# A kernel that plans its own instruction order: casting-queue loads planned to land later, and a longer hold ahead of the next score tile

## The chip, the cores and the metric

One core of one Trainium2 chip. The metric is the device time of one execution in microseconds (us), given as a median over several executions. Engines: PE is TensorE, ACT is ScalarE, DVE is VectorE, POOL is GpSimd, SP is SyncE. A number after an L is a line of the kernel; the change adds one line near the top, so L630 of the kernel before is L631 of the changed one.

## The reference

```python
# q, k, v: (8 batches, 12 heads, 448, 64); x: (3584, 768); w_in: (768, 2048); w_out: (2048, 768); float32
scores = matmul(q, k.T) / 8 - log(448)
attn   = 1 / (1 + exp(-scores))
x      = matmul(attn, v)  # heads put side by side: 3584 x 768
h      = x @ w_in
g      = 0.5 * h * (1 + tanh(sqrt(2/pi) * (h + 0.044715 * h**3)))
out    = g @ w_out
```

## The kernel before

The kernel holds a small scheduler. While it is built, it simulates the engines and the DMA queues with durations of its own, picks at each moment which operation an engine begins next, and then emits one fixed instruction stream for each engine, with semaphores. What the model believes about a load therefore decides the order on the engines, but never when the load really lands. The parts that matter:

```python
DMA_TAIL = 1200.0                      # ns, in the model
...
def drain(self, t):                    # the model's DMA: when a load has landed
    ...
    op.end = self.moved + self.DMA_TAIL + op.late
...
HOLD = 200.0
...
def pe_next(self, t):                  # what PE begins next (first stretch, cut)
    if can and left <= 1 and ...:      # 1. a score tile, if a pair of PSUM banks is free
        return make_qk(n, t)
    soon = trans_ready(t) and ...
    if m and not soon and ...:         # 2. a tile of attention times v
        return av_take(1, t)[0]
    ends = [...]                       #    ends of the ACT tiles under way
    if 0 < n < UB and can and ends and min(ends) < t + HOLD:
        return None                    #    batch 0 only: wait, a bank comes free soon
    if trans_ready(t):                 # 3. the transposes of a q or k
        return make_trans(t)
    return make_part(...) if ...       # 4. a pair of early MLP matmuls
```

Work comes in groups of four heads; three groups are a batch. Groups 0 and 1 load q and k as float32 through the queues of SP and ACT, and DVE or ACT casts them to bf16. From group 2 to group 5 they come through the casting queue of POOL (all loads of v, w_in and w_out too), which converts while it moves. For group 1:

```python
ld[g] = plan.add(Op("ld%s%d" % (nm, g), "AQ" if (nm, g) == ("q", 1) else "SP",
                    lambda e, ap=ap, d=dst[s]: e.dma_start(d[:], ap), ...,
                    pkt=(16, 89.0), late=LATE if g >= PE_TR * NG + NG else 0.0))   # group 1: late = 0
...
cast: deps [ld[g]] + ...               # kb <- kf, qb <- qf
freed[key] = Op("trp%s%s" % (nm, key), "PE", fn, [eye, cast[key], bank_free[bank]], ...)   # transposes
```

The transposes of group 1 stand at a fixed place in PE's stream, between score tiles of group 0. If the load of k for group 1 ("k1" below) is late, PE stops there, and ACT soon has no score tile left.

## Time and profile before

| | before |
|---|---|
| first three runs | median 388.91 us (388.79 to 390.27) |
| the profiled run | 388.43 us, span 386.6 us |
| ACT's 21 sigmoid tiles of batch 0 | 7.06 to 24.65 us |
| run of 24 MLP matmuls in batch 1, start | 55.47 (chain), 55.31 (timeline) |

The chain and the timeline date the same instruction some 0.15 us apart; below, a difference is always taken within one view. The profile itself is read in the prediction.

### The profile page before, as it was taken

What the parts mean: (1) busy time and instruction counts of PE and PEld (TensorE: products, weight loads), DVE (VectorE), ACT (ScalarE), POOL (GpSimd) and SP (SyncE); (2) the same over time, 40 slices, a digit from 0 to 9 for tenths busy, and PEclk for the clock granted to TensorE, in tenths of its full rate; (3) what the DMA queues carried; (4) which work ended last, traced back from release to release, by engine and by line L of the source; (5) the groups of instructions that cost most, each with busy time, mean ns of one, the idle gap of its engine ahead of it and who ended that gap; (6) DMA issues with size and microseconds to landing.
All of it is one profiled execution on the core that took longest, in us unless ns stands there. A gap on an engine that the chain in (4) does not pass through costs nothing.

```text
span 386.6 us, 7500 instructions
## 1 busy us (share of the span) xinstructions
PE 381.8 (99%) x3210; PEld 202.5 (52%) x3210; DVE 155.9 (40%) x273; ACT 227.6 (59%) x337; POOL 53.6 (14%) x84
## 2 busy tenths in 40 slices
PE   8999999999999999999999999999999999999996
PEld 6434445545555555555555555554555545555565
DVE  3446623147680085602864057710767016400000
ACT  5999962268564576546755476645856467543221
POOL 6994110001010111001110011100201000000000
PEclk9999999999999999999999999999999999999999
DMA  8999999747784068903779049940779501110133
GB/s 232 189 203 203 210 207 319 115 88 185 185 209 88 26 164 219 219 0 109 157 203 199 1 120 205 230 72 0 185 184 216 81 0 42 43 41 2 41 83 81
DMA packets 64225, 51.74 MB, mean 134 GB/s; under 512 B 36288, under 2 KB 60736, under 8 KB 64192
## 3 DMA queue, kind: packets, MB, share of 16 engines
q1 hardware_dynamic: 48928, 36.81, 38.9%
q0 software_dynamic: 14560, 13.64, 22.2%
q10 hardware_dynamic: 704, 0.82, 0.7%
q8 instruction: 25, 0.41, 0.4%
q14 instruction: 8, 0.07, 0.1%
HBM read 45.61 MB, written 11.01 MB: 146 GB/s over the span
## 4 chain that ended last, share of the span: by engine, by line
PE 95%; ACT 3%; DVE 0%; issue 0%
PE ps L822 39%; PE ps L777 36%; PE ps L630 9%; PE ps L678 7%; ACT at L641 3%; PE ps L753 2%; PE ps L434 1%; PE ps L587 1%; ACT th L650 0%; PE ps L584 0%; DVE at L654 0%; ACT xT L360 0%; DVE qT L361 0%; ACT ob L360 0%; DVE gT L426 0%
## 5 line engine op out<-in xcount | busy, mean ns | idle before, releaser
L650 ACT ACTIVATE th<-ps 128x896 f32<-128x896 f32 x147 | 126.8, 929 | 44.9 <-PE ps L630 44.8
L822 PE MATMUL ps<-w_out,gT 128*128 128x384 bf16 (+2 forms) x912 | 152.9, 324 | 0.1
L654 DVE TENSOR_SCALAR at<-th 128x896 bf16<-128x896 f32 x147 | 92.2, 628 | 126.3 <-ACT th L650 125.5
L777 PE MATMUL ps<-xT,w_in 128*128 128x448 bf16 x738 | 143.2, 353 | 0.0
L822 PEld LDWEIGHTS ps<-w_out,gT 128*128 128x128 bf16 x912 | 85.9, 98 | 65.5 <-ACT th L650 5.9
L791 ACT ACTIVATE gT<-ps 128x448 bf16<-128x448 f32 x128 | 69.6, 549 | 79.5 <-PE ps L777 78.6
L777 PEld LDWEIGHTS ps<-xT,w_in 128*128 128x128 bf16 x738 | 71.3, 98 | 68.6 <-issue 3.4
L630 PE MATMUL ps<-qT,kT 64*64 64x448 bf16 x672 | 48.3, 359 | 0.5 <-ACT at L641 0.4
L510 POOL DMA_DIRECT2D vb<-in_v_dram x24 | 14.8, 616 | 236.7 <-PE ps L630 233.7
L678 PE MATMUL ps<-at,vb 64*64 64x448 bf16 x672 | 38.2, 350 | 0.2 <-DVE xT L361 0.2
L361 DVE COPY ob<-ps 128x384 f32<-128x384 f32 x43 | 23.8, 554 | 25.1 <-PE ps L822 24.2
L630 PEld LDWEIGHTS ps<-qT,kT 64*64 64x64 bf16 x672 | 15.6, 105 | 25.1 <-issue 11.9
L678 PEld LDWEIGHTS ps<-at,vb 64*64 64x64 bf16 x672 | 19.4, 107 | 12.1 <-issue 1.1
L360 ACT ACTIVATE ob<-ps 128x384 f32<-128x384 f32 (+2 forms) x14 | 6.6, 468 | 25.4 <-PE ps L822 25.4
L361 DVE CAST xT<-ps 128x448 bf16<-128x448 f32 x27 | 16.6, 623 | 10.9 <-PE ps L678 10.9
L512 POOL DMA_DIRECT2D vb<-in_v_dram x24 | 18.8, 785 | 0.2 <-issue 0.2
L641 ACT ACTIVATE at<-ps 128x896 bf16<-128x896 f32 x21 | 17.5, 926 | 0.6 <-PE ps L630 0.5
L361 DVE CAST kb<-kf 128x896 bf16<-128x896 f32 (+2 forms) x21 | 12.6, 599 | 11.4 <-DMA kf<-in_k_dram 10.9
L360 ACT ACTIVATE xT<-ps 128x448 bf16<-128x448 f32 x21 | 11.6, 551 | 1.9 <-PE ps L678 1.9
L361 DVE CAST qb<-qf 128x896 bf16<-128x896 f32 (+1 forms) x20 | 12.2, 608 | 0.7 <-DMA qf<-in_q_dram 0.6
L886 POOL DMA_DIRECT2D w_in<-in_moe_w_in_dram x16 | 10.2, 719 | 0.0
L753 PE MATMUL ps<-xT,w_in 128*128 128x448 bf16 x30 | 7.4, 355 | 0.0
(31 smaller groups left out, 48.2 us busy)
## 6 DMA issues: line engine op xcount, KB each, us to landing
out_dram<-ob SPq DMA_DIRECT2D x54, 192.0 KB, 2.9
kf<-in_k_dram SPq DMA_DIRECT2D x19, 448.0 KB, 4.4
qf<-in_q_dram SPq DMA_DIRECT2D x18, 448.0 KB, 5.6
vb<-in_v_dram POOLq DMA_DIRECT2D x48, 112.0 KB, 5.1
w_out<-in_moe_w_out_dram POOLq DMA_DIRECT2D x4, 768.0 KB, 21.3
w_in<-in_moe_w_in_dram POOLq DMA_DIRECT2D x12, 192.0 KB, 11.3
kb<-in_k_dram POOLq DMA_DIRECT2D x4, 224.0 KB, 8.5
qb<-in_q_dram POOLq DMA_DIRECT2D x4, 224.0 KB, 8.9
```

What stands on the lines that cost most here:

```text
L360: return e.activation(o, i, AF.Copy)
L361: return e.tensor_copy(o, i)
L512: c = plan.add(Op("ldv%db" % g, "SWQ", lambda e, d=dst[64:128], ap=hi: e.dma_start(d, ap), deps, 610.0, 0.0, prio=order_v(g), sem="ldv%db" ...
L630: r = mm(ps[64 * half:64 * half + 64, (x, y)[a], 0:S], kv[d, a, j, :], qv[d, a, :, :], start=True, stop=True)
L641: lambda e: e.activation(at[as_][:], both, AF.Sigmoid, bias=bias, scale=scale),
L650: lambda e: e.activation(th[ts][:], both, AF.Tanh, bias=0.5 * bias, scale=0.5 * scale),
L654: lambda e: e.tensor_scalar(at[as_][:], th[ts][:], 0.5, 0.5, op0=ALU.mult, op1=ALU.add),
L678: r = mm(ps[64 * c:64 * c + 64, banks[a], 0:S], vb[s][d, slot, j, :], at[as_][d, a, :], start=(j == 0), stop=(j == NJ - 1))
L753: r = mm(ps[:, bank, 0:S], w_in[:, kt, fc * 128:(fc + 1) * 128], xT[b][:, kt, :], start=(kt == 0), stop=(kt == KT - 1))
L777: r = mm(ps[:, bank, 0:S], w_in[:, kt, fc * 128:(fc + 1) * 128], xT[xb][:, kt, :], start=(kt == 0), stop=(kt == KT - 1))
L791: lambda e: e.activation(gT[:, fc, col:col + S], ps[:, bank, 0:S], AF.Gelu_apprx_tanh),
L822: r = mm(ps[:, bank, 0:hi - lo], gT[:, fc, col:col + 128], w_out[:, fc, lo:hi], start=(fc == 0), stop=(fc == FC - 1))
```

## The change

It tunes two of the planner's beliefs: loads on the casting queue are taken to land 0.9 us later (so that PE is not planned onto data that is only just there), and in batch 0 PE begins nothing long within 0.3 us of the next free score bank.

```diff
     LATE2 = 500.0
+    LATE3 = 900.0
...
-    HOLD = 200.0
+    HOLD = 300.0
...
-   prio=order_q(g), sem="ldb%s%d" % (nm, s), pkt=(16, 72.0)))
+   prio=order_q(g), sem="ldb%s%d" % (nm, s), pkt=(16, 72.0), late=LATE3))
...     # the same "late=LATE3" on both halves of each v load, and on the w_in and w_out loads
```

More of the change, by code (lines that the diff above doesn't have):

```diff
@@ L510, in load_v @@
             a = plan.add(Op("ldv%da" % g, "SWQ", lambda e, d=dst[0:64], ap=lo: e.dma_start(d, ap),
-                            deps, 610.0, 0.0, prio=order_v(g), sem="ldv%da" % s, pkt=(8, 72.0)))
+                            deps, 610.0, 0.0, prio=order_v(g), sem="ldv%da" % s, pkt=(8, 72.0), late=LATE3))
             c = plan.add(Op("ldv%db" % g, "SWQ", lambda e, d=dst[64:128], ap=hi: e.dma_start(d, ap),
-                            deps, 610.0, 0.0, prio=order_v(g), sem="ldv%db" % s, pkt=(8, 72.0)))
+                            deps, 610.0, 0.0, prio=order_v(g), sem="ldv%db" % s, pkt=(8, 72.0), late=LATE3))
             ld_v[g] = (a, c)
@@ L878, in load_w_in @@
                     w_in_x.append(plan.add(Op("wx%d" % c, "SWQ", lambda e, d=dst, s_=src: e.dma_start(d, s_),
-                                              [], 620.0, 0.0, prio=(1, EARLY.index("x0")), sem="wx%d" % c, pkt=(8, 95.0))))
+                                              [], 620.0, 0.0, prio=(1, EARLY.index("x0")), sem="wx%d" % c, pkt=(8, 95.0), late=LATE3)))
             for c in range(2):
@@ L887, in load_w_in @@
                                            after, 620.0, 0.0, prio=prio,
-                                           sem="wi%d.%d.%d" % (n, c, a), pkt=(12, 80.0) if n else (8, 95.0))))
+                                           sem="wi%d.%d.%d" % (n, c, a), pkt=(12, 80.0) if n else (8, 95.0), late=LATE3)))
             w_in_ld[n] = ops
@@ L894, in load_w_out @@
                                        lambda e: e.dma_start(w_out[:, n * FC // 4:(n + 1) * FC // 4, :], src),
-                                       after, 760.0, 0.0, prio=prio, sem="wo%d" % n, pkt=(32, 117.0)))]
+                                       after, 760.0, 0.0, prio=prio, sem="wo%d" % n, pkt=(32, 117.0), late=LATE3))]
         state = {"n": 0, "av": 0, "queue": [], "a": (0, 0), "b": 0, "h": 0, "avj": 0, "burst": False, "run": 0, "last": ""}
```

## The prediction

> **What bounds the kernel now.** I read the page first, then the chain that ended last in order of time, then each engine's share by stage, then the timelines of ScalarE (ACT) and TensorE (PE) in the first 60 us. The page puts almost the whole span on PE. The windows show that this is not so in the first 20 us.
>
> ```profile
> PE 95%; ACT 3%; DVE 0%; issue 0%
> ...
> 7.00:20.40 13.40, 12.87 (x215) 6.30 (x209) 6.70 (x13) 13.25 (x17) 13.40 (x23) 1.00 1.22 199
> 20.40:55.10 34.70, 34.59 (x367) 15.01 (x368) 19.20 (x32) 31.64 (x48) 15.44 (x23) 1.00 1.21 206
> 55.10:386.60 331.50, 328.55 (x2588) 177.08 (x2586) 127.86 (x223) 180.24 (x270) 21.52 (x30) 1.00 0.54 122
> ```
>
> The columns of the last three lines are stretch, length, then the busy time of PE, weight loads, DVE, ACT and POOL. From 7.0 to 20.4 us ACT is busy 13.25 of 13.40: it makes the sigmoid tiles of batch 0 (line 641, 21 tiles of 128x896), and each needs a score tile (line 630, four matmuls) that PE must have made. From 20.4 us to the end PE is the limit. The chain in order of time (start, us, what) says where it changes hands:
>
> ```profile
> 7.06 5.01 ACT at L641 x6
> 12.06 0.14 issue
> 12.20 0.38 PE ps L630 x4
> 12.58 0.19 PE ps L678 x4
> 12.77 0.51 PE ps L587 x14
> 13.29 0.31 PE ps L630 x4
> 13.60 0.19 PE ps L678 x4
> 13.79 0.51 PE ps L587 x14
> 14.30 0.34 PE ps L630 x4
> 14.64 0.02 issue
> 14.66 5.80 ACT at L641 x7
> 20.46 0.04 issue
> 20.51 0.38 PE ps L630 x4
> ```
>
> Twice in it a score tile (L630) stands behind 14 transposes (L587) of q or k, and ACT then waits for that tile. How much in all:
>
> ```profile
> 7.06 17.59 ACT L641 ACTIVATE at<-ps 128x896 bf16<-128x896 f32 x21 [0.49 <-PE ps L630]
> ```
>
> Narrow windows on this row give the single starts. Undisturbed sigmoids start 0.80 apart. Numbered s0 to s20, s0 starts at 7.06 and s20 at 23.73, so 20 steps took 16.67; at 0.80 they would take 15.96. ACT therefore loses about 0.7 us to late score tiles. The losses sit at s5 (start 11.14, 0.08 late), s8 (13.65, 0.10), s9 (14.66, 0.21), s14 (18.73, 0.06) and s20 (23.73, 0.19). The last one is not a transpose but a pair of early MLP matmuls (L753, 0.48 with the switch) ahead of the tile:
>
> ```profile
> 22.52 0.36 PE L678 MATMUL ps<-at,vb 64*64 64x448 bf16 x4
> 22.81 0.55 PE L753 MATMUL ps<-xT,w_in 128*128 128x448 bf16 x2
> 23.29 0.38 PE L630 MATMUL ps<-qT,kT 64*64 64x448 bf16 x4
> ```
>
> **What the Trainium skill says.** "Perfetto Trace Analysis", Optimization Strategy, says that the contended engine can change between regimes and that one looks for the gaps of that engine inside its regime; the same page, Identifying the Most-Contended Engine, says that matmul busy time is no good measure. The trace agrees: PE shows 12.87 of 13.40 busy in a stretch where it waits for ACT. "TensorEngine Tiling (Array Packing)", Key Properties, says that a change of tiling mode drains TensorE. Here six MLP matmuls before a score tile take 1.24 us in the chain and twelve take 2.38, so six cost 1.14 (0.19 each) and the change of mode costs the 0.10 left over; starts of single matmuls put it at 0.094. "DMA: Bandwidth & Descriptors", Anatomy of one DMA, gives about 2 us fixed per load and says most of it is completion; here the page has 5.1 us (median) from issue to landing for the v loads, as up to four dozen loads queue. No run yet shows whether a later assumed landing is nearer the truth.
>
> **The change, part by part.** Nothing that runs is added or removed on purpose: the kernel plans its own order at build time, and the change moves two numbers of that plan. LATE3 lets the plan believe that each load on the casting queue lands 0.9 us later, and HOLD (200 to 300 ns) forbids PE to begin a transpose or an early MLP pair in batch 0 when an ACT tile will end, and so free a score bank, within 0.3 us. I compared the instruction order of the two programs. DMA queues: identical. DVE and ACT: one tanh tile moves past gelus early in batch 1, and likewise at its end; one affine step moves across an eviction. PE: the rows differ from the 16th to the 88th; after that the order is the same to the last instruction, that is from 55.12 us on. So LATE3 does nothing to loads after that point, and only the first 55 us can change. There the new order (a) puts one more warm-up matmul (+0.05) where the first attention-times-v tile stood; (b) makes the score tiles of s9, s10 (one before the q transposes instead of both after), s14 and s16 go ahead of the transposes; (c) takes the MLP pair out from ahead of the tile of s20; (d) merges runs of MLP matmuls, with 50 instead of 52 changes of mode by the 55 us point (counted row by row).
>
> Working through it with durations from the trace (score or attention tile 0.19, change of mode 0.094, 14 transposes with change 0.51, sigmoid 0.80 apart and 0.92 long, a score tile 0.43 to 0.44 before its sigmoid):
> - s5: its tile follows the warm-up directly, at 10.57; s5 at 11.06 instead of 11.14.
> - s8: the k transposes still stand ahead of its tile; it stays 0.10 late, at 13.57 (was 13.65).
> - s9: its tile starts when s7 ends, 13.63; s9 at 14.38 (was 14.66). s10 15.18, s11 15.98 (was 16.28): gain 0.30.
> - s12: the next attention tiles wait for DVE's eviction of the previous ones, which barely moves (15.17 before, 15.09 now); then two of them, the score tile of s11, one more and the MLP pair stand ahead, so the tile of s12 starts at 16.46 and s12 at 16.89 (was 17.07). That is a new stall of 0.11; gain down to 0.18.
> - s14 18.50 (was 18.73); s16 20.11 (was 20.34); s18 21.71 (was 21.94), gain 0.23.
> - s19 22.57, a stall of 0.06 behind the MLP pair that remains; s20 23.38 (was 23.73), gain 0.35.
> - PE: the first tanh score tile at 23.66 (was 24.28), but two MLP matmuls (2 x 0.19) and two changes of mode are still owed; the last attention tile of batch 0 waits for s20 to end at 24.30, then ten to twelve MLP matmuls follow. The second tanh tile's scores start at 26.51 against 26.63. There both kernels have done the same work: gain 0.12.
> - From there to 55.12 PE stands almost without a gap in both, with the same matmuls, and 23 changes of mode against 25: 2 x 0.094 = 0.19.
> Sum: 0.12 + 0.19 = 0.31 us. The remaining 331.5 us are the same instructions in the same order at PE's pace, so the end comes 0.3 us earlier: 388.91 - 0.3 = 388.6 us, 0.08%.
>
> **The rivals.**
> 1. ACT takes the gain back in batch 1. After the second tanh tile (27.07) ACT runs without a gap until 41.10, where it waits 0.66 us for PE. By the walk its second tanh starts only 0.08 earlier (26.99), while PE would be up to 0.3 earlier, so score tiles could wait for a bank. For it: the fourth tanh's bank frees at 31.22 by my walk and PE asks for it at 31.25. Against: the new order hands ACT one tanh fewer before the first big attention block, and the old one shows no PE wait for ACT there beyond the change of mode. It would leave 0.1 us of gain: 388.8.
> 2. The later assumed landing idles PE for nothing: v0 lands at 9.87 us, before 10.5 where the old order uses it, so the warm-up put in its place is 0.05 of waste, and similar holds could cost a few tenths. Against it: PE has slack in that stretch. It would make 389.1.
> 3. The losses of ACT vanish wholly (0.7 us) and PE follows: 388.2. Against it: s12 and s8, and PE's owed MLP work.
> 4. A load that really lands late stalls PE. The old trace has transposes of group 4 starting at 29.40 with their loads landing at 28.38 and 29.49 (k, q; q is used at 29.8): 0.3 of margin. The new order uses them after six more MLP matmuls, about 30.2, so the margin grows. The first wi slices land at 21.48 and were used at once (21.82); now their first use is about 23.2. This may be the use of LATE3, but the old wait was short. w_out lands at 56.80, 3 us ahead of its use at 59.85, so starting 0.3 earlier is safe.
>
> **Range and chances.** Every rival lies between 388.2 and 389.1. Three runs of the kernel before spread from 388.79 to 390.27, so a median of three may move a few tenths by itself. Range 388.1 to 389.3. Two per cent is 7.8 us; only 55 us of the program are touched and ACT's whole loss there is 0.7, so same has 0.985.
>
> **What would show it.** Right: sigmoids that start 0.80 apart at s9, s14 and s20, with single stalls of 0.1 at s8 and s12; 21 tiles in about 17.25 us (was 17.59); the run of 24 MLP matmuls of batch 1's second part at about 55.2 instead of 55.47 in the chain; from there on the same durations; a span of about 386.3. Wrong: more than 0.1 us of PE waiting for ACT between 27 and 45 us (rival 1), a new wait for a casting load, or a shift of the later stretch in length by more than 0.2 us, which no order explains.

## The result, and the profile after

Six runs of the changed kernel had a median of 389.8 us (388.37 to 390.21). The kernel before, over its six runs by then, had 389.2 (388.79 to 390.27). The ratio of the fast runs is 1.0005, with an interval of 0.9983 to 1.0026: the same. Here and below, a ratio is the mean time of one kernel's fast runs over that of the other's of the same rounds, so it is not quite the ratio of the medians quoted.

The profiled run of the changed kernel took 389.86 us, span 388.1. The page's chain shares, and the windows of the same three stretches as before (columns: stretch, length, busy time of PE, weight loads, DVE, ACT, POOL, then granted clock, DMA share and GB/s):

```profile
PE 93%; ACT 2%; DMA 2%; DVE 1%; SPq 0%; issue 0%
```

```profile
7.00:20.40 13.40, 11.38 (x190) 5.84 (x184) 5.52 (x10) 11.93 (x15) 13.40 (x23) 1.00 1.22 208
20.40:55.10 34.70, 34.54 (x394) 15.69 (x392) 19.77 (x33) 32.53 (x48) 14.82 (x24) 1.00 1.21 206
55.10:388.10 333.00, 329.96 (x2604) 177.53 (x2592) 128.45 (x224) 180.78 (x271) 21.50 (x30) 1.00 0.54 121
```

DMA has appeared in the chain with 2%, and both PE and ACT were busy about 1.4 us less in the first stretch. The chain in order of time names the load:

```profile
2.27 7.75 DMA kf<-in_k_dram
...
10.04 0.80 DVE kb L362
...
10.89 0.56 PE ps L585 x7
11.45 0.34 PE ps L631 x4
...
11.82 7.62 ACT at L642 x9
```

The load of k1 was issued at 2.27 us, as in the kernel before, and landed at 10.02. Before, it had landed at 8.35. DVE's cast, PE's seven transposes (L585) and the next score tile (L631) follow directly, and ACT resumes at 11.82. ACT's own rows show the hole:

```profile
7.20 3.35 ACT L642 ACTIVATE at<-ps 128x896 bf16<-128x896 f32 x4 [0.49 <-PE ps L631]
11.82 14.24 ACT L642 ACTIVATE at<-ps 128x896 bf16<-128x896 f32 x17 [1.27 <-PE ps L631]
```

The fifth sigmoid starts 2.20 us after the fourth instead of 0.80: a stall of 1.40 us. The row says that ACT waited for PE; PE's rows show that PE had itself been waiting for the cast (1.46 us), and the cast for the load (1.88 us):

```profile
10.04 0.79 DVE L362 CAST kb<-kf 128x896 bf16<-128x896 f32 x1 [1.88 <-DMA kf<-in_k_dram]
...
10.89 0.56 PE L585 MATMUL ps<-ident,kb 128*128 128x128 bf16 x7 [1.46 <-DVE kb L362]
```

In the kernel before, the same cast had waited much less, and the transposes not at all:

```profile
8.37 0.63 DVE L361 CAST kb<-kf 128x896 bf16<-128x896 f32 x1 [0.35 <-DMA kf<-in_k_dram]
```

The 24 matmuls of batch 1 start at 56.89 us in the chain (55.47 before), and from there to the end both kernels take the same time: 331.2 us (388.1 - 56.89), before 331.1 (386.6 - 55.47). So the longer span comes wholly from before that point, and the stall of 1.40 us is nearly all of it.

The change cannot have made this load late. The DMA queues hold the same loads in the same order in both kernels, and PE's stream is the same past these transposes and those of q (by the recorded count its rows differ from the 16th on). The trace's single packets show two of this load that took 1.34 and 0.94 us, where 0.07 is usual; whether such packets are the cause is taken up under "Open" below. The first theory, then: **k1 lands at a different time in each execution; it stalls both kernels alike, and the one profile of before that the prediction was built on, like the three runs behind it, was lucky.** The rival, called X where the expectations give it a letter: something in the changed program itself makes it lose. The expectations call the first theory L; their C (the new order costs time by itself) and X (it makes a late load dearer) are two forms of this rival, and J says that the lateness sits elsewhere.

### The profile page after: what moved, and what is told of

The parts are those of the page before. It is cut to its first block, busy times and chain, and to the rows that moved or that the text cites. A ratio compares the mean times of both kernels' runs of the same rounds, so it can differ in the third digit from the quotient of the medians.

```text
span 388.1 us, 7505 instructions
## 1 busy us (share of the span) xinstructions
PE 381.3 (98%) x3211; PEld 203.0 (52%) x3211; DVE 155.7 (40%) x273; ACT 227.7 (59%) x337; POOL 52.8 (14%) x84
## 4 chain that ended last, share of the span: by engine, by line
PE 93%; ACT 2%; DMA 2%; DVE 1%; SPq 0%; issue 0%
PE ps L823 39%; PE ps L778 36%; PE ps L631 9%; PE ps L679 7%; DMA kf<-in_k_dram 2%; ACT at L642 2%; PE ps L754 2%; PE ps L588 1%; SPq L488 0%; DVE xT L362 0%; ACT th L651 0%; DVE kb L362 0%; DVE at L655 0%; DVE kT L362 0%; PE ps L585 0%
## 5 line engine op out<-in xcount | busy, mean ns | idle before, releaser
L631 PE MATMUL ps<-qT,kT 64*64 64x448 bf16 x672 | 48.1, 358 | 0.5 <-ACT at L642 0.4
L631 PEld LDWEIGHTS ps<-qT,kT 64*64 64x64 bf16 x672 | 15.7, 105 | 24.5 <-issue 11.0
```

Of the source, the lines that this page charges most:

```text
L631: r = mm(ps[64 * half:64 * half + 64, (x, y)[a], 0:S], kv[d, a, j, :], qv[d, a, :, :], start=True, stop=True)
```

## The experiments

Four jobs, sixteen kernels, all correct. Each job timed the kernel before on the same chip; its medians were 389.38, 389.76, 389.46 and 389.49 us.

### The two kernels again, unedited

`after_again` and `after_again2` are the changed kernel, `before_again` is the kernel before, with no edit at all.

> The changed kernel, not edited, timed again beside the kernel before. Theory L (landing): both kernels pay 1:1 for an early k load of group 1 that lands later than about 8.7 us, which differs from execution to execution; so both show times from 388.4 to 390.3, and the fastest of this kernel lie 0.3 to 0.5 us below the fastest of before. In the profile, sigmoid s4 to s5 are more than 0.9 us apart only if that load landed after 8.7. Rival C (order): the new order itself costs time, and all runs stay above the fast ones of before (over 389.3) whatever the landing.

> The changed kernel unedited, third time. So far its 12 runs have a median of 389.70 and the 39 runs of the kernel before 389.46. Theory L with chance alone: against the before runs of this job between -0.4 and +0.2 us. Rival X (the new order makes late landings dearer): again 0.2 or more above.

> The kernel before unedited, as a run of its own, for a second profile of it. If its k load of group 1 lands after 8.7 us, the gap from s3 to s4 or s4 to s5 holds the lateness one for one, as in the changed kernel; the arrival at the 24 matmuls of batch 1, less that stall, should be 55.4 to 55.6 us.

Measured: 389.55 (ratio 1.0008, 0.999 to 1.0026), 389.24 (0.9987, 0.9966 to 1.0009) and 389.14 (0.9985, 0.9962 to 1.0007). Not all came as expected: the fastest run of `after_again` was to lie 0.3 to 0.5 us below the fastest of before, and lay 0.28 above it (389.13, 388.85). But the kernel before stalls as well. ACT's rows in the profile of `before_again`:

```profile
7.45 3.35 ACT L641 ACTIVATE at<-ps 128x896 bf16<-128x896 f32 x4 [0.58 <-PE ps L630]
11.40 14.49 ACT L641 ACTIVATE at<-ps 128x896 bf16<-128x896 f32 x17 [0.61 <-PE ps L630]
```

and the wait of PE that stands behind it (us in total, times, longest):

```profile
PE ps L584 <- DVE kb L361: 0.8, 1, 0.8
```

Put side by side, the profiled executions order themselves, to within 0.02 us, by this one stall (how far the fifth sigmoid starts beyond 0.80 us after the fourth):

| profile | k1 landed, us | stall, us | time of that run, us |
|---|---|---|---|
| before | 8.35 | 0 | 388.43 |
| after_again2 | 9.31 | 0.47 | 389.03 |
| before_again | 9.77 | 0.75 | 389.68 |
| after_again | 9.75 | 0.94 | 389.66 |
| after | 10.02 | 1.40 | 389.86 |

The stall is the larger part, but not all: in the order of the table the first sigmoid started at 7.06, 7.34, 7.45, 7.25 and 7.20 us. Stall and later start together give the times above the first row to within 0.15 us. The later start is also why `before_again` missed its expectation for the 24 matmuls (55.4 to 55.6 us without the stall; 56.73 - 0.75 = 55.98 in the chain).

A copy of the kernel before came out 0.15% under its own twin, so a difference of that size between two sets of six runs says nothing. All runs of all jobs together: before, 56 runs, median 389.46, mean 389.59, standard deviation 0.68; changed, 18 runs, median 389.55, mean 389.58, deviation 0.63. The difference of the means is 0.01, with about 0.36 (twice 0.66 x sqrt(1/18 + 1/56)) to either side. The five runs above 391.2 (four of before, one of the changed kernel) are the ones in which the mean granted clock was 0.996; without them the means are 389.45 and 389.48, 0.03 apart with 0.27 to either side. Only 15 of the 56 runs of before lie under 389.1, yet two of the first three did, so their median of 388.91 stood some 0.5 us low. Rival X finds no support here.

### A dose of the suspected cause: a load put ahead of k1

```diff
+        k1 = next(op for op in plan.order["SP"] if op.name == "ldk1")
+        k1_load = k1.fn
+        def behind(e):     # 448 columns of float32 = 224 KB; the ..late192 kernels take 192 = 96 KB
+            e.dma_start(spare[:], k[2, 0:4]...[:, 0:448]).then_inc(held, 16)   # nobody reads spare
+            return k1_load(e)
+        k1.fn = behind
```

> The kernel before, with one more load of 224 KB into a buffer that nobody reads, issued ahead of the k load of group 1. At about 200 GB/s it takes 1.1 us. Theory L: the k load lands at about 9.5 us, s4 to s5 are about 1.7 us apart (0.80 and 0.9 of waiting), and the time is about 389.8, the level of the slower runs. Rival J: the wait is absorbed and the time stays at 388.9 to 389.2.

> The kernel before with a load of 96 KB (not 224) that nobody reads ahead of the k load of group 1, a dose small enough to keep PE's idle time under about 1.5 us. The k load should land at about 9.3 us. Theory L: time rises by the delay beyond 8.7, that is 0.6 us over the fast level, with the spread of chance on top: median 389.5 to 390.2.

> The changed kernel with the same 96 KB dose. Theory L: the stall is the same as in the kernel before, and the gain behind it stays 0.1 to 0.4, so 0.1 to 0.4 us below the dosed kernel before. Rival X (exposure: the new order makes a late load dearer, because it keeps less work free ahead of the wait): 0.2 us or more above the dosed kernel before.

Measured: `before_k1late` 391.13 us (ratio 1.0049, 1.0021 to 1.0077). k1 landed at 10.45, not at the 9.5 expected; the next sigmoids started 2.99 and 1.75 us after their forerunners, so they lost 2.2 + 0.95 us. Making k1 late makes the kernel slow: that direction is shown. The time was to be 389.8; it cost more than the delay alone, as PE's granted clock fell after the wait (window columns as above; the clock is the third figure from the end):

```profile
10.00:11.00 1.00, 0.00 (x0) 0.00 (x0) 0.53 (x1) 0.50 (x1) 1.00 (x2) 1.00 1.24 194
11.00:12.00 1.00, 0.84 (x11) 0.65 (x11) 0.64 (x2) 0.00 (x0) 1.00 (x3) 0.65 1.26 202
12.00:13.00 1.00, 1.00 (x10) 0.62 (x11) 0.62 (x1) 0.44 (x1) 1.00 (x2) 0.50 1.26 200
13.00:14.00 1.00, 1.00 (x12) 0.47 (x13) 0.59 (x1) 0.48 (x1) 1.00 (x3) 0.50 1.23 194
14.00:15.00 1.00, 1.00 (x20) 0.53 (x16) 0.03 (x1) 0.69 (x1) 1.00 (x3) 0.65 1.21 173
```

Half speed for the 3.4 us seen here makes a mean clock of about 0.996 over 390 us (an estimate: 1 - 1.7/390), and three of the six runs had a mean clock of 0.996 or 0.991. That the slowest runs of the unedited kernels, at 0.996, had such a wait too fits, but none of them was profiled.

The small dose scattered widely: 390.51 for before (388.99 to 392.57; ratio 1.0018, 0.9985 to 1.0052) and 390.53 for the changed kernel (388.76 to 393.25; 1.0022, 0.9985 to 1.0059). The changed one was to be 0.1 to 0.4 us lower; with this spread that is not decided. The equal medians give X no support either. Five of the twelve runs had a clock of 0.996 or 0.991. In the profile of before k1 landed at 10.34, not at the 9.3 expected, the sigmoids lost 1.84 and 0.95 us, and the clock fell as above. In the profile of the changed one k1 landed at 9.10, the stall was 0.40, and that run took 388.76.

### Less of the suspected cause: q of group 1 behind k1 on SP's queue

```diff
         plan.run()
+        q1 = next(op for op in plan.order["AQ"] if op.name == "ldq1")
+        behind = next(i for i, op in enumerate(plan.order["SP"]) if op.name == "ldk1") + 1
+        plan.order["AQ"].remove(q1)
+        q1.eng, q1.deps = "SP", []
+        plan.order["SP"].insert(behind, q1)
```

The two loads then no longer run against each other, and both kernels get the same edit.

> The kernel before, with the q load of group 1 issued on the same queue behind the k load, not on a second queue beside it; instruction order of PE, ACT's arithmetic and DVE unchanged. Theory L: the k load lands at about 7 us, not 8.35, and has over 1.5 us to spare, q still at about 9; the high times vanish: all five within 0.6 us, at 388.5 to 389.2. Rival C says nothing of it. Rival J (jitter elsewhere): the spread stays 1.3 us or more.

> The same edit in the changed kernel. Theory L: all five within 0.6 us and 0.3 to 0.5 us below the same edit of before (388.1 to 388.8); sigmoids 0.80 apart from s4 to s5. Rival C: still over 389.3, or at least no faster than the same edit of before.

Measured: 388.98 for before (ratio 0.9989, 0.9976 to 1.0001), 388.64 for the changed kernel (0.9977, 0.9965 to 0.999). k1 landed at 8.34 and 8.16: no sooner than in the lucky profile, so the hope of about 7 was a miss. But the stall at the fifth sigmoid was gone, and a smaller one appeared at the sixth (0.37 and 0.40 us), since q now lands at 9.71 and 9.81. (That of before also lost 0.60 us at the 13th, where PE waited 0.56 for a slice of w_in.) The same pair was run again, with each half of the change alone on the same base:

```diff
-    HOLD = 200.0
+    HOLD = 300.0        # hold_only_k1first; late3_only_k1first has LATE3 and its uses instead
```

> The kernel before with q of group 1 behind k on one queue, once more (388.76 to 389.56 the first time): the base on which the two parts of the change are now tried on one chip, since its spread is the smallest. Median 388.8 to 389.2.

> That base with HOLD at 300 alone. Its order still has the MLP pairs and score tiles of batch 0 otherwise as before, and 126 changes of mode as before, not 124. Theory (the score tiles that no longer stand behind transposes or MLP pairs are the gain): 0 to 0.3 us under the base, mostly at s16 to s20. Rival (the gain is LATE3's): equal to the base within 0.1.

> That base with LATE3 at 900 alone. The transposes of group 2 and the score tiles around s9 move as in the full change, but the order has 130 changes of mode, 6 more than the full change (about 0.6 us at 0.094 each, of which part lies where PE waits anyway). Theory: -0.1 to +0.4 us against the base. Rival (the gain is LATE3's): 0.3 us under the base.

> That base with both, the whole change, again: 0.2 to 0.5 us under the base, as the first time (388.64 against 388.98). Rival C (the change gains nothing once landings are equal): within 0.1 of the base.

Measured: base 389.39 (388.83 to 391.18), HOLD alone 390.0 (389.39 to 390.82), LATE3 alone 389.74 (389.15 to 390.26), both 388.83 (388.51 to 389.4). The base missed its 388.8 to 389.2, and HOLD alone its 0 to 0.3 under the base. The parts do not add up: neither gains alone, and together they come out 0.56 us under the base. With five or six runs each, only the steps from one part to both are clear of the noise (means 1.09 and 0.75 us apart, with 0.56 and 0.50 to either side); the base against any of the three is not (0.8 to 0.9 to either side). PE's waits between 6 and 30 us show what each profile lacks. With HOLD alone:

```profile
PE ps L753 <- DMA w_in<-in_moe_w_in_dram: 0.9, 1, 0.9
...
PE ps L587 <- DMA kb<-in_k_dram: 0.5, 1, 0.5
```

and in the base, `before_k1first_b`:

```profile
PE ps L584 <- DVE qb L361: 0.9, 1, 0.9
...
PE ps L587 <- DMA qb<-in_q_dram: 0.2, 1, 0.2
PE ps L587 <- DMA kb<-in_k_dram: 0.2, 1, 0.2
```

The first line of the base has nothing to do with the change: q of group 1 landed at 10.65, and ACT lost 1.17 us at the sixth sigmoid. In the four profiles of this job k1 landed between 7.72 and 9.09 us and q between 9.64 and 10.65, and the base's runs spread over 2.35 us, which is the sign that was set for rival J. So the edit moved the chance to q rather than ending it. The other lines are loads of the casting queue. With LATE3, alone or with HOLD, these profiles have no such wait (of the other profiles with it, one, `after_again`, shows 0.2 us for a v load). But LATE3 alone switches PE's mode 130 times in its order, against 126 for HOLD alone and 124 for both. Six switches more are about 0.56 us at the 0.094 us that one took here; that fits part of the 0.91 between LATE3 alone and both, and no run tested it by itself.

### The planner told about k1

If loads of group 1 vary, the planner can be told to take them to land later too, which moves their transposes back and leaves the data alone.

```diff
-   late=LATE if g >= PE_TR * NG + NG else 0.0))
+   late=LATE if g >= PE_TR * NG + NG else 800.0 if g == 1 else 0.0))     # or 1500.0
```

> The changed kernel, with the k and q loads of group 1 planned 0.8 us later as well. In PE's order this puts the score tile qk0.4 ahead of the k transposes of group 1, and qk0.5 ahead of the q transposes; DMA order unchanged. Theory L: the k load is then needed about 0.8 us later (10.0), so the 1.0 to 1.4 us stalls between s3 and s4 fall to 0 to 0.5; median 388.5 to 388.9, clearly under the changed kernel's 389.5 of the earlier job, and spread 0.8 or less. Rival J (the lateness hits anywhere and this spot is not special): median stays at 389.3 to 389.7.

> The same with 1.5 us: qk0.4 and qk0.5 both stand ahead of the k transposes. Theory L: k is needed 1.6 us later than in the changed kernel (about 10.8), no stall is left at s4 in ordinary executions; 388.3 to 388.8, unless the transposes of group 1, now nearer to their use at s7, make it wait up to 0.3 us. Rival J: 389.3 to 389.7.

Measured: 389.73 with 800 (ratio 1.0, 0.9973 to 1.0027) and 389.27 with 1500 (0.9982, 0.996 to 1.0005). Both were misses, and both teach. With 800, the plan had put the cast of q ahead of that of k on DVE, since in the model both wait anyway. In this execution q landed last:

```profile
10.56 0.63 DVE L362 CAST qb<-qf 128x896 bf16<-128x896 f32 x1 [2.17 <-DMA qf<-in_q_dram]
11.10 0.63 DVE L362 CAST kb<-kf 128x896 bf16<-128x896 f32 x1
11.79 0.56 PE L585 MATMUL ps<-ident,kb 128*128 128x128 bf16 x7 [1.33 <-DVE kb L362]
```

k1 had been there since 10.13, but its cast stood behind that of q. With 1500, the six runs lie within 0.26 us (389.16 to 389.42), the narrowest of all, which is what the theory asks for when the load's luck is taken out. But the transposes now stand so near their use that in the one profile ACT loses 0.8 us at the eighth sigmoid, though k1 had landed at 8.75. (The casts are swapped there too.)

Then the same 800 with the order of the casts fixed, on both kernels:

```diff
+   [ld[g]] + ... + (later(cast_k, 1) if (nm, g) == ("q", 1) else [])     # q's cast of group 1 behind k's
```

> The changed kernel with the loads of group 1 planned 0.8 us later, and the k cast kept ahead of the q cast on DVE (in the first try DVE took q first and k waited for it, 0.5 us). Theory L: with k landing at 8.4 no stall, at 10.0 only about 0.4 to 0.6; median 388.5 to 389.0 and spread under 1.0. Rival J: 389.4 or more.

> The same two edits in the kernel before. Theory L: also under the unedited kernel, 388.8 to 389.3, and 0.1 to 0.5 above the edited changed kernel.

Measured: the changed kernel with it took **388.72 us (388.19 to 389.01), ratio 0.9969, 0.9946 to 0.9992**, the best ratio of all: 0.3% under before, which is real by its interval and still "the same" at 2%. Under the changed kernel of the same job its mean lies 0.65 us (0.35 to either side). In its profile k1 landed at 9.14, as late as where `after_k1late192` had stalled by 0.40, and no sigmoid lost more than 0.12 us:

```profile
7.24 17.21 ACT L642 ACTIVATE at<-ps 128x896 bf16<-128x896 f32 x21 [0.49 <-PE ps L631]
```

This profile gave part of it back at 69 us: there PE waited 0.57 us for a copy on DVE that stood behind the cast of a later k load, for which DVE had itself waited 0.53. From the 24 matmuls to the end it took 332.1 us, where the other profiles have 331.3 to 331.5.

The kernel before with the same edit had 389.21 (0.9986, 0.9963 to 1.001). It had no stall at the fifth sigmoid either (0.42 at the sixth), but PE waited for the first slices of w_in, and ACT's 20th sigmoid came 1.28 us late:

```profile
PE ps L753 <- DMA w_in<-in_moe_w_in_dram: 1.2, 1, 1.2
```

This is what LATE3 can do: with the stall of k1 out of the way, the casting queue's loads can be the next to stall. They need not be: in the first profile of before the slice had landed at 21.48, 0.34 us ahead of its use; here it came at 23.46. The old order uses the w_in slices right after the attention tile av2.2, the new one only after av2.4. The three pairs on equal bases:

| base | old order, median | both parts, median | difference |
|---|---|---|---|
| q behind k1 | 388.98 | 388.64 | -0.34 |
| q behind k1, again | 389.39 | 388.83 | -0.56 |
| group 1 taken 800 ns later, casts in order | 389.21 | 388.72 | -0.49 |

Pooled, 17 runs each: mean 389.35 with deviation 0.68, against 388.73 with deviation 0.31. On these bases the change gains about 0.6 us (the means are 0.62 apart, with 0.36 to either side) and halves the spread; in the unedited pair, where the stall of k1 stands before it, nothing of this shows.

## Why the prediction was right or wrong

**Within 2%: right.** Only the first 55 us could change, and so it was.

**The time: wrong.** 388.6 with a range up to 389.3 against 389.8. The failed step is the subtraction "388.91 - 0.3" with the start of its walk: it took k1 to land where the one profile had it, so s0 to s4 stood 0.80 apart as a matter of course. In the profile after, s4 came 1.40 us late. Taken from the median of all 56 runs, 389.46, the same 0.31 gives 389.15. The six runs of the changed kernel then fell on the high side of that (its 18 runs: 389.55).

**The range: wrong in the same way.** Three runs "may move a few tenths": with a deviation near 0.65 for one run, medians of small sets did move that much. Three runs were too few to show it, but the hint was there: the profiled run of before, at 388.43, already lay 0.36 below the lowest of them.

**Rival 4 named the right kind of cost and looked at the wrong load.** It asked for margins from the casting loads, which the change names. It did not ask for that of k1, a plain load that stands just ahead of ACT's stretch, and whose cast had waited 0.35 us for it even in the lucky profile. The cast ended at 9.00 and PE began the transposes at 9.21: with 0.2 us of slack, nearly each tenth of lateness passes on.

**The walk through ACT's stalls: right in kind, its gain too large.** The predicted stalls came: 0.10 at s8, 0.10 at s12 (0.11 predicted), 0.10 at s19 (0.06 predicted), none at s9, s14 and s20. Two were missed: s5 lost 0.07 (its tile follows the warm-up), and s15 lost 0.10 behind the k transposes of group 3. Without the k1 stall, s20 came 16.54 us after s0 (17.94 - 1.40), where the walk has 16.32 and before had 16.67. So ACT gained 0.13, not 0.35. One reading beside the walk was wrong: the "four dozen" v loads are the page's count for the whole run; at most 16 loads of the casting queue were under way at once.

**From there to batch 1.** Take 1.40 of stall and 0.15 of later start (7.20 against 7.06) off the changed kernel's chain. Its second tanh tile's scores then start at 26.84, against 26.70 before in the same view: 0.14 later, where the prediction had 0.12 earlier. The stretch to the 24 matmuls is 28.50 us instead of 28.77, a gain of 0.27, where two mode changes fewer were to give 0.19. In sum 0.13, not 0.31. Two views of other executions agree: by the timeline, corrected alike, the 24 matmuls start at 55.19 in after, 55.18 and 55.17 in the repeats, and 55.31 in before. In `before_again` it is 55.42, so the gain lies between 0.12 and 0.25.

**Rival 1 (ACT takes the gain back in batch 1): not seen;** PE waits for ACT nowhere there, and ACT's one longer wait is 0.66 us in both kernels. **Rival 3 (ACT's losses vanish wholly): not seen;** without the stall of k1, 16.54 us for 20 steps is still 0.58 above 15.96. **Rival 2 (the assumed lateness idles PE for nothing): not seen as a cost;** on equal bases it takes waits away. That the measured gain there (0.34 to 0.56) is above the walk's 0.13 fits those waits of 0.4 to 1.4 us in the old order and with HOLD alone, none of which the prediction counted. It rests on one profile of each kernel, and in the second base the larger wait was that for q.

**Open:** why k1 sometimes lands late. Slow packets alone do not decide it: in `before_k1late192` it landed at 10.34 with no packet over 0.6 us, in `before_k1first` at 8.34 although six packets on the queue that carries it and q of group 1 took 0.7 to 1.25. The difference is in the tail: half of k1's 256 packets had ended by 6.02 us in before and 6.08 in after, the last at 7.70 and 9.38. In the unedited pair, a gain of the size predicted is neither shown nor excluded, as the 0.36 to either side covers it (without the runs at 0.996, 0.03 and 0.27, the 0.31 lies just outside and the 0.13 within).

## What to carry to other kernels

Before taking a few tenths off a median, ask how far single runs lie apart and which load of the profile was used with next to no slack; a profile is one execution, and an engine with a fixed order passes on nearly each tenth by which such a load is late. Let a planner's assumed lateness cover the first load that can stall: here, guarding the later ones showed nothing while the earlier stall stood. When an assumed time is changed, read the new order on every engine: here it silently swapped two casts on DVE, and the gain showed only once they were put back in order.

## What the Trainium skill lacked or had wrong

- "DMA: Bandwidth & Descriptors", Latency and other measured facts, gives the access to HBM as 0.2 us on average and 2 us at high load. A packet's time in the trace is not that latency itself; single packets took 1.34 and 0.94 us against a usual 0.07. What the page lacks is how far a whole load can move from one execution to the next: with the same program up to that point, the same 448 KB load landed between 8.35 and 10.02 us over five executions, and the stall behind it was up to 1.40 us.
- "TensorE: Matmul & The Clock Gate", Part 1, What's actually happening, ties the drop to half clock to an idle window of about 3.4 us, free-running (further down, the page also names frequent short pauses). Here a single wait of PE of 1.78 us (`before_k1late`; 1.65 in `before_k1late192`) was enough: from about 11.3 us the granted clock was 0.50, for some 3.4 us. A wait of 1.46 us left it at 1.00. The two values, 1.0 and 0.5, agree with the page; whether the phase of the window or the busy share within it decides is not shown.
- "TensorEngine Tiling (Array Packing)", Key Properties, says that a change of mode drains TensorE but gives no figure; here it took 0.094 us.
